# A fused delta-rule attention and MLP kernel: another order at the beginning, weights fetched at once and split in another way, the first two units' layers run jointly by halves of the weights

## The chip, the cores and the metric

The kernel runs on one core of a Trainium2 chip. The metric is the device time of one execution in microseconds, median over runs. The engines of the core are named as in the profile: PE (TensorE matmuls; PEld its weight loads), DVE (VectorE), ACT (ScalarE), POOL (GpSimd) and SP (SyncE, which issues most DMAs).

## The reference

For each batch and head a state of 48 x 48 is updated token by token by the delta rule, and the outputs go through two dense layers with a squared ReLU between them:

```python
k_n = k / (np.linalg.norm(k, axis=-1, keepdims=True) + 1e-06)
for t in range(S):
    kt, vt, bt = (k_n[:, :, t], v[:, :, t], beta[:, :, t, None])
    y[:, :, t] = np.einsum('bhd,bhde->bhe', q[:, :, t], state)
    v_old = np.einsum('bhde,bhd->bhe', state, kt)
    state = state + bt[:, :, :, None] * np.einsum('bhd,bhe->bhde', kt, vt - v_old)
h = np.maximum(x @ w_in, 0.0)          # x: y with its heads joined, (3072, 384)
return (h * h @ w_out).astype(np.float32)
```

There are 4 batches, 8 heads, 768 tokens and a head width of 48. `w_in` is 384 x 2048 and `w_out` 2048 x 384, both of 64-bit floats; q, k, v and beta are 32-bit. 12.6 MB of weights have to be read and turned into 32-bit numbers.

## The kernel before

**Units.** The work is cut into 12 units: 128 tokens of two batches, unit u being the token block u // 2 of batch pair u % 2. Inside a unit the tokens come in chunks of 64, and the token recurrence of a chunk is replaced by the inverse of a triangular matrix. Units of the same pair follow each other through `state`; the first two units (0 and 1) begin with a state of zero.

**What a unit goes through.** `load`, `load_v`, `load_q`, `load_beta` fetch its tokens over SP. `normalize` scales k. `static` transposes k and q and forms the masked products `ap`, which go through DRAM (`blocks`) into the layout `lt`. `invert` solves 31 steps on DVE, one pair of operations each (L347, L350), and sends the result over DRAM (`inv`) into `tt` and `t1t`. `whole` joins the halves of the inverse, `applied` multiplies it with k and v, and `sequential` carries the state over the two chunks and writes y. `moe` feeds y transposed into `x_h`, `x_l` (the number as a rounded part and a remainder, since the matmuls take rounded fp32), runs the first layer in 8 double blocks of 256 columns (two pieces of 9 matmuls each, L665), takes relu, square and the two parts on ACT and DVE (L672 to L675, `h_l` L644), and the second layer two double blocks later (two pieces of 6 matmuls of 384 each, L652), accumulated in the two banks `o0` and `o1`.

**Weights.** There are 28 parts: for each quarter of the 2048 columns three of `w_in` (128 x 512) and four of `w_out` (128 x 384). `split_weights` turns the two 32-bit words of each 64-bit number into a rounded high part and a rest: ACT takes the absolute value of the upper word (L145), DVE runs five operations (L146 to L154), ACT rounds the high part (L160), PE forms number minus high part plus lower bits as a sum of three matmuls (L165 to L167), and ACT copies it back as the rest (L168). The low step of one weight is written behind the high step of the next.

**Order.** The order of PE, SP, DVE and ACT is written out by hand: each part of the work is a generator, `take` runs some steps of one, and `weave` mixes several by positions between 0 and 1, with the layers as filler between steps of attention. The program begins with `first_pair` (units 0 and 1 together, with halves of 16 steps in the solve and products written into unused weight tiles), splits placed between its steps by `take(splits, 1)`; then `applied` and `sequential` of both units; then one `weave` per unit u from 1 to 11. Weave u has `static` of u + 1 in its first fifth, the state part of u from 0.34 on, most of `invert` of u + 1 from 0.40 on, the layers of u - 1 throughout, and in u = 1 the rest of the splits up to 0.88. SP's queue is in the order written, too. Weights are fetched in pieces between q, v and k of the first units, the last 13 (L130 by `fetch(NW)`) once the tiles that `first_pair` borrowed are free.

Of the kernel before, what the change touches and what calls it, by code (L numbers as in the profile page):

```python
# [16 lines left out]
LEAST = 2.0 ** -15  # L17
# [3 lines left out]
def kernel(  # L21
# [74 lines left out]
    ttall = const.tile([P, NU, NC, H, C], F32, name="tt")  # L96
    ttile = [ttall[:, i] for i in range(NU)]
# [24 lines left out]
    AHEAD = 10  # L122
# [10 lines left out]
    def room(x, n):  # L133
        pool, first, second = rooms[x % 2 if x < AHEAD else 0]
        return pool.tile([P, PC], I32, name=first)[:, :n], pool.tile([P, PC], I32, name=second)[:, :n]

    def split_weights():


        def words(x):  # L140
            raw = raws[x]
            w1 = raw[:, :, 1]
            a, rest = room(x, w1.shape[1])

            nc.scalar.activation(out=a.bitcast(F32), in_=w1.bitcast(F32), func=AF.Abs)  # L145
            nc.vector.tensor_scalar(out=a.bitcast(F32), in0=a.bitcast(F32), scalar1=LEAST, scalar2=None, op0=ALU.max)  # L146
            nc.vector.tensor_scalar(out=a, in0=a, scalar1=3, scalar2=0x3FFFFFF8,
                                    op0=ALU.logical_shift_left, op1=ALU.bitwise_and)

            nc.vector.scalar_tensor_tensor(out=a, in0=w1, scalar=-0x40000000, in1=a,  # L150
                                           op0=ALU.bitwise_and, op1=ALU.bitwise_or)

            nc.vector.tensor_scalar(out=w1, in0=a, scalar1=-0x800000, scalar2=None, op0=ALU.bitwise_and)  # L153
            nc.vector.scalar_tensor_tensor(out=rest.bitcast(F32R), in0=raw[:, :, 0].bitcast(U32), scalar=2.0 ** -52,  # L154
                                           in1=w1.bitcast(F32), op0=ALU.mult, op1=ALU.mult)
            return x, a, rest

        def high(x, a, rest):
            hl = wpool.tile([P, 2, raws[x].shape[1]], F32R, name=place[x])
            nc.scalar.copy(out=hl[:, 0], in_=a.bitcast(F32))  # L160
            return x, a, rest, hl

        def low(x, a, rest, hl):
            ps = split_bank()[:, :hl.shape[2]]
            nc.tensor.matmul(ps, lhsT=ident, rhs=a.bitcast(F32), start=True, stop=False)  # L165
# [3 lines left out]
            halves[weight_parts[x][:2]] = hl[:, 0], hl[:, 1]  # L169
# [160 lines left out]
    def invert(d):  # L330
# [21 lines left out]
        nc.vector.tensor_tensor(out=z, in0=z, in1=bt.unsqueeze(1).broadcast_to([P, J, HB]), op=ALU.mult)  # L352
        inv = dram.tile([4, H2, HB, HB], F32, name="inv")
# [12 lines left out]
    def first_pair(ds):  # L366
# [6 lines left out]
        chs = [(i, c, 2 * p + j, j, i * NX + c * NP + p) for i in range(2) for c in range(NC) for p in range(NP) for j in range(2)]  # L373

        def wide(x, *shape):
            return wpool.tile([P, *shape], F32, name=place[x])

        def all_heads(t):
            return ttall[:, :, :, :, t].rearrange("p u c h t -> p (u c h) t")

        bt = apool.tile([P, 2, HS], F32, name="btp", bufs=1)
        for r in range(2):
            for j in range(2):
                for half in range(2):
# [13 lines left out]
        yield

        def transposed(d, c, which):  # L400
            tp = x_tile(0).rearrange("p (n t) -> p n t", n=NP)
            for p in range(NP):
                nc.tensor.transpose(tp[:, p], d["qp" if which else "kp"][:, c, 2 * p:2 * p + 2].rearrange("p a b -> p (a b)"),
                                    ident)
            nc.scalar.copy(out=d["kq"][:, c, :, :, which], in_=tp.rearrange("p n (b t) -> p n b t", b=2))

        def blocks(across):

            ps = [x_tile(0).rearrange("p (i t) -> p i t", t=HB) for _ in range(2)]
            for i, d in enumerate(ds):  # L410
                for x in range(NX):
                    for half in range(2):
                        for r in range(2):
                            for j in range(2):
                                block = d["kq"][j * C:j * C + D, x // NP, x % NP, r, 0].rearrange("d (f t) -> d f t", f=2)
                                nc.tensor.matmul(ps[j][quarter[2 * r + half], i * NX + x], lhsT=block[:, half],
                                                 rhs=block[:, half ^ across], start=True, stop=True)
            return ps

        for d in ds:  # L420
            for c in range(NC):
                transposed(d, c, 0)
        yield
        near = blocks(0)
        yield
        f = apool.tile([P, 2, HS, 2, HS], F32, name="lt", bufs=1)
        gs = wide(NW - 7, 2, 2 * NX, HB)
        for j in range(2):
# [5 lines left out]
        for j, ps in enumerate(blocks(1)):  # L434
            nc.scalar.copy(out=os[:, j], in_=ps)
        yield
        for d in ds:
            for c in range(NC):
                transposed(d, c, 1)
# [419 lines left out]
```

## Time and profile before

| what | value |
|---|---|
| time, median of 3 runs | 744.1 us (741.33 to 745.07) |
| profiled execution, its own time | 744.84 us |
| its span, first to last instruction | 743.1 us |
| mean granted TensorE clock | 0.931 |
| PE busy | 660.0 us (89%) |
| DVE busy | 429.0 us (58%) |
| ACT busy | 335.2 us (45%) |
| POOL busy | 48.1 us (6%) |

Busy time is the union of an engine's instructions. Matmuls are pipelined and their ends are modelled, so a busy PE is not always a PE at its peak, and shares over the whole span mix stages with different limits; the granted clock of a slice tells of PE's pace there. In a group of instructions the fields are line, engine, operation, out<-in by tile names, shape, count, busy us and mean ns of one, and the idle time just before them with what ended it.

### The profile page before, as it was taken

How to read it: one execution, taken by the hardware profiler on the slowest of the kernel's cores; microseconds unless marked ns; L12 is line 12 of the kernel's file. 1: busy time of each engine (PE TensorE's matmuls, PEld its weight loads, DVE VectorE, ACT ScalarE, POOL GpSimd, SP SyncE). 2: the span in 40 equal slices, each digit the busy share in tenths (PEclk: the TensorE clock that was granted, in tenths of full speed). 3: DMA queues.
4: the chain of work that ended last, by engine and by line, in shares of the span. 5: the costliest groups of instructions: out<-in, count | busy, mean ns of one | idle time of the engine just before them, and what ended most of it. 6: DMA issues, size and time to landing. Idle time of an engine off the chain costs nothing.

```text
span 743.1 us, 25321 instructions
## 1 busy us (share of the span) xinstructions
PE 660.0 (89%) x11000; PEld 610.3 (82%) x11000; DVE 429.0 (58%) x1168; ACT 335.2 (45%) x623; POOL 48.1 (6%) x85
## 2 busy tenths in 40 slices
PE   2626876787689999999999999999999999999997
PEld 2415755566579999999999999999999999999997
DVE  3585146447774675764937748558476494661211
ACT  3321443544445535455444454553545534545352
POOL 8321100000001001010010100100101001000000
PEclk9775578788699999999999999999999999999999
DMA  8672700050003415324153142341532414111000
GB/s 176 168 182 53 279 6 2 4 93 12 1 1 65 94 26 100 54 46 98 28 100 67 26 98 49 52 100 25 105 57 36 99 35 93 33 29 32 3 21 21
DMA packets 164462, 47.71 MB, mean 64 GB/s; under 512 B 156416, under 2 KB 159488, under 8 KB 164352
## 3 DMA queue, kind: packets, MB, share of 16 engines
q1 hardware_dynamic: 160992, 45.48, 29.5%
q8 instruction: 86, 1.41, 0.8%
q10 hardware_dynamic: 2336, 0.59, 0.4%
q0 software_dynamic: 1024, 0.03, 0.1%
q14 instruction: 24, 0.20, 0.1%
HBM read 36.01 MB, written 9.96 MB: 62 GB/s over the span
## 4 chain that ended last, share of the span: by engine, by line
PE 80%; DVE 11%; ACT 4%; issue 3%; DMA 1%; SPq 0%; DVEq 0%; ACTq 0%
PE h L665 28%; PE o L652 27%; PE g L572 3%; PE g L596 3%; PE x L565 2%; PE x L609 2%; PE g L617 2%; PE o L165 1%; DVE a L150 1%; PE x L295 1%; DVE rest L154 1%; PE g L295 1%; DVE w L153 1%; PE g L285 1%; PE x L285 1%
## 5 line engine op out<-in xcount | busy, mean ns | idle before, releaser
L652 PE MATMUL o<-w,h_h 128*128 128x384 f32 x768 | 202.6, 345 | 0.0
L665 PE MATMUL h<-x_h,w 128*128 128x256 f32 x1152 | 177.5, 291 | 4.0 <-ACT w L168 3.1
L665 PEld LDWEIGHTS h<-x_h,w 128*128 128x128 f32 x1152 | 158.2, 194 | 10.0 <-ACT w L168 3.4
L644 DVE TENSOR_TENSOR h_l<-r,h_h 128x512 fp32r<-128x512 f32 x96 | 66.3, 691 | 149.4 <-PE o L652 68.6
L652 PEld LDWEIGHTS o<-w,h_h 128*128 128x128 f32 x768 | 133.2, 189 | 2.3
L672 ACT ACTIVATE r<-h 128x512 f32<-128x512 f32 x96 | 57.4, 598 | 171.3 <-PE h L665 171.0
L652 PE MATMUL o<-w,h_l 128*128 128x384 f32 x384 | 129.6, 337 | 0.0
L347 DVE SCALAR_TENSOR_TENSOR tmp<-lt,bt,z 128x126 f32<-128x126 f32 (+22 forms) x310 | 95.5, 308 | 23.6 <-DMA out_dram<-a 11.9
L665 PE MATMUL h<-x_l,w 128*128 128x256 f32 x576 | 101.1, 285 | 0.0
L350 DVE TENSOR_TENSOR z<-z,tmp 128x126 f32<-128x126 f32 (+22 forms) x310 | 79.2, 255 | 10.6
L665 PEld LDWEIGHTS h<-x_l,w 128*128 128x128 f32 x576 | 83.9, 194 | 0.0
L652 PEld LDWEIGHTS o<-w,h_l 128*128 128x128 f32 x384 | 72.2, 188 | 0.0
L673 ACT ACTIVATE r<-r 128x512 f32<-128x512 f32 x96 | 60.6, 632 | 3.1
L675 ACT CAST h_h<-r 128x512 fp32r<-128x512 f32 x96 | 59.5, 620 | 3.0
L160 ACT CAST w<-a 128x384 fp32r<-128x384 f32 (+1 forms) x23 | 12.7, 553 | 80.7 <-DVE rest L154 80.7
L338 POOL MEMSET z<- 128x512 f32 x10 | 5.3, 526 | 534.5 <-DMA inv<-z 478.0
L596 PEld LDWEIGHTS g<-state,kq 48*64 48x64 f32 x1408 | 24.3, 142 | 9.1 <-ACT a L145 4.5
L596 PE MATMUL g<-state,kq 48*64 48x48 f32 x1408 | 27.0, 228 | 5.1 <-ACT a L145 4.4
L146 DVE TENSOR_SCALAR a<-a 128x384 f32<-128x384 f32 (+1 forms) x23 | 8.8, 385 | 39.2 <-ACT a L145 39.2
L165 PE MATMUL x<-a,plus 128*128 128x384 f32 (+1 forms) x36 | 18.4, 597 | 13.3 <-DVE a L150 9.7
L240 DVE TENSOR_REDUCE n<-rest 128x8 f32<-128x384 f32 x20 | 10.9, 550 | 28.9 <-ACT rest L239 28.9
L551 ACT ACTIVATE tt<-x 32x256 f32<-32x256 f32 x40 | 15.0, 374 | 25.7 <-PE x L547 25.3
(171 smaller groups left out, 816.3 us busy)
## 6 DMA issues: line engine op xcount, KB each, us to landing
w<-in_moe_w_in_dram SPq DMA_DIRECT2D x12, 512.0 KB
w<-in_moe_w_out_dram SPq DMA_DIRECT2D x16, 384.0 KB
lt<-blocks SPq DMA_DIRECT2D x20, 256.0 KB
vt<-in_v_dram SPq DMA_DIRECT2D x96, 48.0 KB
out_dram<-a SPq DMA_DIRECT2D x46, 96.0 KB
kpad<-in_k_dram SPq DMA_DIRECT2D x88, 48.0 KB
qpad<-in_q_dram SPq DMA_DIRECT2D x88, 48.0 KB
blocks<-ap SPq DMA_DIRECT2D x40, 64.0 KB
```

The costliest lines, as they stand in the source:

```text
L165: nc.tensor.matmul(ps, lhsT=ident, rhs=a.bitcast(F32), start=True, stop=False)
L347: nc.vector.scalar_tensor_tensor(out=tmp, in0=lt[:, s:s + 1, s + 1:].broadcast_to([P, nj, nt]), scalar=bt[:, s:s + 1], op0=ALU.mult, op1=A ...
L350: nc.vector.tensor_tensor(out=z[:, :nj, s + 1:], in0=z[:, :nj, s + 1:], in1=tmp, op=ALU.subtract)
L551: nc.scalar.mul(out=right[upper[b], j, :, HB:], in_=ps[j][upper[b]], mul=-1.0)
L572: nc.tensor.matmul(g[rows, c, h], lhsT=tt[rows, c, h], rhs=vt[rows, c, h], start=True, stop=True)
L596: nc.tensor.matmul(dst[to * C:(to + 1) * C, j, p], lhsT=kq[rows, c, p, b, x], rhs=s[rows, b, p], start=(x == 0 and p == 0), stop=False, sk ...
L644: nc.vector.tensor_tensor(out=h_l, in0=r, in1=h_h.bitcast(F32), op=ALU.subtract)
L652: nc.tensor.matmul(o[i], lhsT=a[:, e, i * P:(i + 1) * P], rhs=halves["wo", ft][w], start=(ft == 0 and n == 0), stop=(ft == FT - 1 and n == 2))
L665: nc.tensor.matmul(hp[:, e], lhsT=halves["wi", (kt, ft // EACH)][w][:, f], rhs=x[:, kt], start=(n == 0), stop=(n == 3 * KT - 1))
L672: nc.scalar.activation(out=r, in_=hp, func=AF.Relu)
L673: nc.scalar.activation(out=r, in_=r, func=AF.Square)
L675: nc.scalar.copy(out=h_h, in_=r)
```

## The change

**Tiles.** `tt` is no longer a constant but a tile of the attention pool, made anew by `new_tt`: once for units 0 and 1, then its place holds `x1` (the layers' input of unit 1), then it is made again in the last step of `invert` of unit 2. The places of `first_pair` move out of the weights' tiles into others (`vt`, `h_h`, `x_h`, `x_l`), so no weight's fetch waits for them.

**Fetch.** All weights are issued on SP before v of units 0 and 1: 4 after k, 3 after q of unit 0, the rest after q of unit 1. v follows once `inner` has read the places it shares.

**Split.** ACT's step (`begin`) is issued two weights ahead and scales down, which replaces the `max` on DVE and lets one sign bit be merged instead of two. The first 6 weights still take PE's sum, with 4 operations on DVE. For the other 22, six operations on DVE form the rest directly, and PE and the second copy on ACT go.

```diff
-    ttall = const.tile([P, NU, NC, H, C], F32, name="tt")
-    ttile = [ttall[:, i] for i in range(NU)]
+    ttile = []
+
+    def new_tt():
+        tt = apool.tile([P, NU, NC, H, C], F32, name="tt", bufs=1)
+        ttile[:] = [tt[:, i] for i in range(NU)]
+        return tt
...
     def split_weights():
...
+        def words(x, sums):
+            a, rest = started[x]
+            n = a.shape[1]
+            w0, w1 = [raws[x][:, :, i] for i in range(2)]
+            nc.vector.tensor_scalar(out=a, in0=a, scalar1=3, scalar2=0 if sums else 1,
+                                    op0=ALU.logical_shift_left, op1=ALU.bitwise_or)
+            nc.vector.scalar_tensor_tensor(out=a, in0=w1, scalar=-0x80000000, in1=a,
                                            op0=ALU.bitwise_and, op1=ALU.bitwise_or)
...
+            else:
+
+                nc.vector.tensor_scalar(out=rest, in0=w0, scalar1=9, scalar2=None, op0=ALU.logical_shift_right)
+                nc.vector.scalar_tensor_tensor(out=rest, in0=w1, scalar=23, in1=rest,
+                                               op0=ALU.logical_shift_left, op1=ALU.bitwise_or)
+                hl = wpool.tile([P, 2, n], F32R, name=place[x])
+                power = apool.tile([P, PC], I32, name="t1", bufs=1)[:, :n]
+                nc.vector.tensor_scalar(out=power, in0=a, scalar1=-0x800000, scalar2=None, op0=ALU.bitwise_and)
+                nc.vector.scalar_tensor_tensor(out=hl[:, 1], in0=rest, scalar=2.0 ** -43, in1=power.bitcast(F32),
+                                               op0=ALU.mult, op1=ALU.mult)
             nc.scalar.copy(out=hl[:, 0], in_=a.bitcast(F32))
...
         before = None
+        begin()
+        begin()
+        yield
         for x in range(NW):
-            now = high(*words(x))
-            yield
+            sums = x < SUMS
+            now = words(x, sums)
             if before:
                 low(*before)
+            before = now if sums else None
+            if x + 2 < AHEAD:
+                begin()
+            if x >= AHEAD - 3:
                 yield
-            before = now
-        low(*before)
-        yield
...
+            if x + 2 >= AHEAD:
+                begin()
+            yield
```

**First pair.** It is cut into functions that are called one by one with `piece` (a split) between them. `blocks(1)`, the second pass of 256 small products, goes: `products` now multiplies k with k and q at once, and `outer` takes the block from `ap`. Beta comes by 8 DMAs and a transpose instead of 32. The masks of `ap` on POOL come after `outer`, and POOL's order is written by hand too.

**Joint layers.** The layers of units 0 and 1 run in four runs over halves of the weights: unit 0 with the first half (its sums are copied to `kept`, a tile in one of the two places of `vt`), unit 1 with the first and then the second half, and unit 0 with the second half, where `kept` is added. Of its 68 steps 50 stand in weave 1 and the rest in weave 2; weave 3 goes on with unit 2 alone as before. `invert` of unit 2 stands wholly in weave 1, from 0.5 to 0.9, and the rest of the splits up to 0.66.

```diff
+    def joint(d0, d1, x0, x1, kept):
+
+        def keep(o):
+            nc.scalar.copy(out=kept[:, 0], in_=o[0])
+            nc.vector.tensor_copy(out=kept[:, 1], in_=o[1])
+            yield
+
+        first, second = list(range(FT // 4)), list(range(FT // 4, FT // 2))
+        return layers([(d0, x0, first, keep), (d1, x1, first, None), (d1, x1, second, lambda o: results(d1, o)),
+                       (d0, x0, second, lambda o: results(d0, o, kept))])
...
+        x1 = apool.tile([P, 2, KT, 2 * P], F32R, name="tt", bufs=1)
+        x1 = [x1[:, 0], x1[:, 1]]
+        take(feed(ds_[1], x1))
         take(third)
-        split_early = False
+        kept = apool.tile([P, 2, DM], F32, name="vt", bufs=2)
         before = inverse = None
+        both = joint(*ds_[:2], x0, x1, kept)
         n_i = round((1 - I0) / (I1 - I0) * NI)
+        NJ, NF, NS = 68, 50, 2 * (NW - AHEAD + 3) - 16
         for u in range(1, units):
-            parts = [(splits, NS, 0, 0.88, "quiet")] if u == 1 else []
+            parts = [(splits, NS, 0, 0.66, "quiet")] if u == 1 else []
...
+            if u == 1:
+                parts.append((both, NF, M0, M1, ""))
+            elif u == 2:
+                parts.append((both, NJ - NF, 0, M1, ""))
```

**How the order moves.** On PE, where the first layer begins, before: `gy` of unit 1's state (L617), the sums of one weight (L165 to L167: number, high part, lower bits), then the 9 matmuls of a piece.

```order
L617 MATMUL g<-r,ap 64x48 x16
L165 MATMUL x<-a,plus 128x384
L166 MATMUL x<-w_1636,minus 128x384
L167 MATMUL x<-rest,plus 128x384
L665 MATMUL h<-x_h,w_296 128x256
L665 MATMUL h<-x_h,w_436 128x256
L665 MATMUL h<-x_h,w_451 128x256
```

And now, with the transposes of y of unit 1 (L668) in place of the sums:

```order
L654 MATMUL g<-r,ap 64x48 x16
L668 MATMUL h<-plus,y 128x128 x6
L735 MATMUL h<-x_h,w_282 128x256
L735 MATMUL h<-x_h,w_364 128x256
L735 MATMUL h<-x_h,w_447 128x256
```

The three matmuls of the sum are gone from here on, and the feed of unit 1, which stood in weave 2, has moved ahead of all layers.

On DVE, one weight of 384 columns in weave 1 and what stands next to it; before (`a` the words, `rest` the lower bits, `h_l` the remainder of the layers' middle values):

```order
L146 TENSOR_SCALAR a<-a 128x384
L147 TENSOR_SCALAR a<-a 128x384
L150 SCALAR_TENSOR_TENSOR a<-w_236,a 128x384
L153 TENSOR_SCALAR w_236<-a 128x384
L154 SCALAR_TENSOR_TENSOR rest<-w_236 128x384
L644 TENSOR_TENSOR h_l<-r,h_h 128x512
```

And now:

```order
L154 TENSOR_SCALAR a<-a 128x384
L156 SCALAR_TENSOR_TENSOR a<-w_202,a 128x384
L165 TENSOR_SCALAR rest<-w_202 128x384
L166 SCALAR_TENSOR_TENSOR rest<-w_202,rest 128x384
L170 TENSOR_SCALAR t_1722<-a 128x384
L171 SCALAR_TENSOR_TENSOR w_1721<-rest,t_1722 128x384
L704 TENSOR_TENSOR h_l<-r,h_h 128x512
```

One operation more stands ahead of the same `h_l`, and the last one writes the weight's rest itself.

On SP, v and q in weave 2 (units 3 and 4), with the semaphores each DMA waits for; before:

```order
L199 DMA kpad_102<-in_k_dram 64x4x48 [waits DMAHW6_49]
L199 DMA kpad_102<-in_k_dram 64x4x48 [waits DMAHW7_49]
L199 DMA vt<-in_v_dram 64x4x48 [waits DMAHW0_49]
L199 DMA vt<-in_v_dram 64x4x48 [waits DMAHW1_49]
L199 DMA vt<-in_v_dram 64x4x48 [waits DMAHW2_49]
```

And now:

```order
L215 DMA kpad_102<-in_k_dram 64x4x48 [waits DMAHW6_49]
L215 DMA kpad_102<-in_k_dram 64x4x48 [waits DMAHW7_49]
L215 DMA vt<-in_v_dram 64x4x48 [waits DMAHW0_49,DVE_49,Activation_49]
L215 DMA vt<-in_v_dram 64x4x48 [waits DMAHW1_49]
L215 DMA vt<-in_v_dram 64x4x48 [waits DMAHW2_49]
```

The order is the same, but the first DMA of v has a wait for DVE and ACT that it had not: of the two places of `vt` one is held by `kept`, and unit 2 uses the other.

More of the change, by code (lines that the diff above doesn't have):

```diff
@@ L513, in first_pair @@
[L513 to L522 removed]
+        return dict(betas=betas, sides=sides(), transposed=transposed, near=near, blocks=blocks, products=products,
+                    solve=solve(), inner=inner, joined=joined, halves_done=halves_done, outer=outer, last=last, masks=masks)
@@ L636, in moe, with xs_tiles, results, layers @@
             yield
-        o = [ps_o.tile([P, PC], F32, name=f"o{i}")[:, :DM] for i in range(2)]
-        hs, later = [], []
+    def xs_tiles():
+        return [mpool.tile([P, KT, 2 * P], F32R, name=n, bufs=1) for n in ("x_h", "x_l")]
+    def results(d, o, kept=None):
+        if kept is not None:
+            for c in range(2):
+                nc.vector.tensor_tensor(out=kept[:, c], in0=kept[:, c], in1=o[c], op=ALU.add)
+            done = [kept[:, c] for c in range(2)]
+        else:
+            done = []
+            for c in range(2):
+                done.append(spool.tile([P, PC], F32, name="a")[:, :DM])
+                (nc.vector.tensor_copy if c else nc.scalar.copy)(out=done[c], in_=o[c])
+        yield
+        for c in range(2):
+            for b in range(2):
+                row = (d["b0"] + b) * S + d["t0"] + c * C
+                queue = nc.scalar if d["u"] == units - 1 and c == 0 else nc.sync
+                queue.dma_start(out=out[row:row + C], in_=done[c][b * C:(b + 1) * C])
+    def layers(runs):
+        work = [(run, fp) for run in range(len(runs)) for fp in runs[run][2]]
+        later, o = [], []
         def rest():
@@ L644, in rest, with second @@
                 nc.vector.tensor_tensor(out=h_l, in0=r, in1=h_h.bitcast(F32), op=ALU.subtract)
-        def second(fp):
-            h_h, h_l = hs[fp]
+        def second(run, fp, h_h, h_l):
+            _, _, fps, end = runs[run]
+            if fp == fps[0] and (run == 0 or runs[run - 1][3]):
+                o[:] = [ps_o.tile([P, PC], F32, name=f"o{i}")[:, :DM] for i in range(2)]
+                begins = True
+            else:
+                begins = False
             for e in range(2):
@@ L652, in second @@
                         nc.tensor.matmul(o[i], lhsT=a[:, e, i * P:(i + 1) * P], rhs=halves["wo", ft][w],
-                                         start=(ft == 0 and n == 0), stop=(ft == FT - 1 and n == 2))
+                                         start=(begins and e == 0 and n == 0),
+                                         stop=(bool(end) and fp == fps[-1] and e == 1 and n == 2))
                 rest()
                 yield
-        for fp in range(FT // 2):
+            if end and fp == fps[-1]:
+                yield from end(list(o))
+        waiting = []
+        for run, fp in work:
+            x_h, x_l = runs[run][1]
             hp = ps_h.tile([P, PC], F32, name="h").rearrange("p (e t) -> p e t", e=2)
```

478 lines of the change are left out of this document (253 added, 225 removed).

## The prediction

> **What bounds the kernel now.** I read the page first, then the busy time by stretches. In the page's slices the granted TensorE clock is low and uneven over about the first twelve, and full after them:
>
> ```profile
> PEclk9775578788699999999999999999999999999999
> ```
>
> I cut the span at three places of the program: the first matmul of `applied` for unit 0, the first matmul of the first layer, and the end of the first weave (u = 1). The first two stand in the timeline of PE (start, length, line):
>
> ```profile
> 84.44 0.36 PE L565 MATMUL h<-tt,kpad 64*64 64x64 f32 x1
> ...
> 124.62 0.87 PE L665 MATMUL h<-x_h,w 128*128 128x256 f32 x6
> ```
>
> Busy time in these stretches (length, then each engine's busy us and count, the clock, DMA share and GB/s):
>
> ```profile
> 0.00:84.40 84.40, 40.64 (x1460) 33.03 (x1460) 43.51 (x90) 26.54 (x50) 30.56 (x58) 0.72 0.63 164
> 84.40:124.60 40.20, 31.04 (x675) 24.02 (x671) 19.59 (x46) 16.94 (x33) 0.00 (x0) 0.70 0.16 55
> 124.60:226.60 102.00, 76.32 (x420) 63.20 (x419) 68.04 (x171) 45.00 (x89) 0.00 (x0) 0.85 0.11 20
> 226.60:743.10 516.50, 511.98 (x8454) 490.02 (x8452) 297.85 (x861) 246.68 (x452) 17.59 (x27) 1.00 0.31 57
> ```
>
> Call them A, B, C and D. D is TensorE's alone: 512.0 of 516.5 us at clock 1.00. A, B and C last 226.6 us, with PE busy for 148.0 and below full clock; no engine is full there, chains through PE, ACT and DVE set the pace. So the change can gain in two ways: less work in D, or shorter chains in A to C.
>
> **Prices.** Warm matmuls and the period of the steady stage, from the chain of waits (start, us, what):
>
> ```profile
> 247.82 1.85 PE g L572 x64
> ...
> 264.25 2.11 PE o L652 x12
> ...
> 275.54 2.12 PE h L665 x18
> ...
> 296.33 1.85 PE g L572 x64
> ```
>
> A unit has 144 first-layer and 96 second-layer matmuls: 144/18 x 2.12 + 96/12 x 2.11 = 33.9 us, or 1.06 us for each of its 32 pieces. The period is 296.33 - 247.82 = 48.5 us, so attention takes 14.6.
>
> **D, work taken out.** What stood before the cut at 226.6 is seen in C's groups of matmuls, and in PE's timeline just before it:
>
> ```profile
> L665 PE MATMUL h<-x_l,w 128*128 128x256 f32 x51 | 10.9, 333 | 0.0
> ...
> L652 PE MATMUL o<-w,h_l 128*128 128x384 f32 x31 | 10.6, 343 | 0.0
> ```
>
> ```profile
> 223.10 0.60 PE L285 MATMUL g<-plus,qpad 128*128 128x128 f32 x4
> ```
>
> At 3 and 2 to a piece these are 17 first-layer and 16 second-layer pieces (one record is missing): 33 of 384 are done, 351 left, 372 us. The change's first weave runs 50 of the 68 steps of the joint layers, one of them the copy to `kept`, so 49 pieces; 335 are left, 355 us. That is 17 less in D, paid for in C; but unit 3's transposes, four groups like the row above, some 2 us, fall into D now. So -15.
>
> **C, the first weave.** PE's own work there is now 49 x 1.06 = 52 plus about 6 for `static` of unit 2 (part of the 14.6): 58. A weight's split cost it this (a cold one, then a warm one, each with the matmul that follows):
>
> ```profile
> 105.70 2.07 PE L165 MATMUL o<-r,plus 128*128 128x512 f32 x2
> ...
> 108.65 0.25 PE L609 MATMUL x<-r,kpad 64*64 64x48 f32 x1
> ...
> 163.86 0.81 PE L165 MATMUL x<-a,plus 128*128 128x384 f32 x2
> ...
> 164.86 0.34 PE L652 MATMUL o<-w,h_h 128*128 128x384 f32 x1
> ```
>
> So 1.00 to 2.95 us, for all 28 weights; now 6 have it. In C the splits leave PE altogether, and with them PE's waits for ACT's and DVE's half of each. The price goes to DVE, whose groups in C, shapes apart, read (count | busy, mean ns):
>
> ```profile
> L150 DVE SCALAR_TENSOR_TENSOR a<-w,a 128x384 int32<-128x384 int32 x11 | 6.1, 558 | 0.4
> ...
> L150 DVE SCALAR_TENSOR_TENSOR a<-w,a 128x512 int32<-128x512 int32 x6 | 4.2, 693 | 0.2
> ...
> L153 DVE TENSOR_SCALAR w<-a 128x384 int32<-128x384 int32 x11 | 4.0, 361 | 0.4
> ...
> L153 DVE TENSOR_SCALAR w<-a 128x512 int32<-128x512 int32 x6 | 2.6, 428 | 0.2
> ...
> L304 DVE TENSOR_TENSOR ap<-x,mask 128x512 f32<-128x512 f32 x2 | 1.3, 682 | 0.0
> ```
>
> ```profile
> L347 DVE SCALAR_TENSOR_TENSOR tmp<-lt,bt,z 128x126 f32<-128x126 f32 (+22 forms) x31 | 9.5, 306 | 0.5
> L350 DVE TENSOR_TENSOR z<-z,tmp 128x126 f32<-128x126 f32 (+22 forms) x31 | 7.9, 255 | 1.1
> ...
> L644 DVE TENSOR_TENSOR h_l<-r,h_h 128x512 fp32r<-128x512 f32 x8 | 5.5, 690 | 8.3 <-PE o L652 7.4 <-ACT h_h L675 0.8
> ```
>
> An old split is 2 such STTs and 3 TENSOR_SCALARs: 2.20 us (384) or 2.67 (512). A new one without sums is 3 and 3: 2.76 or 3.36. The shifts have no row; as TENSOR_SCALARs of the same shape I give them L153's. So the "fewer operations" hold for PE and ACT, not for DVE. Twelve weights (four of 512, eight of 384) remain for C: 13.4 + 22.1 = 35.5. To it come 13 `h_l` x 0.69 = 9.0, four masks of 0.68 = 2.7, the inversion of unit 2, now whole in C (17.4), and some 4 for norms and copies: about 69 against PE's 58. The weave puts the splits into its first 0.66 and the inversion into 0.5 to 0.9, so up to 0.66 DVE has 35.5 + 6 + 2.7 + 7 = 51 against PE's 38, then PE's 20 bounds: 71. I take 78, a tenth more for hand-overs. Bounds: 62 if DVE runs ahead, 97 if PE keeps its old ratio of 61 us of such work (35 layers, 20 splits, 6 static) in 102.
>
> **A, the beginning.** Rows of DVE and POOL around the solve:
>
> ```profile
> 39.32 0.36 DVE L146 TENSOR_SCALAR r<-r 128x384 f32<-128x384 f32 x1 [5.71 <-ACT r L145]
> ...
> 44.87 1.01 DVE L471 TENSOR_TENSOR z<-z,tmp 128x30 f32<-128x30 f32 x1
> ...
> 51.53 0.29 DVE L471 TENSOR_TENSOR z<-z,tmp 128x128 f32<-128x128 f32 x1
> ```
>
> ```profile
> 43.24 5.08 POOL L454 TENSOR_SCALAR_AFFINE_SELECT ap<-ap 64x1024 f32<-64x1024 f32 x4 [17.82 <-ACT ap L451]
> ```
>
> The 5.71 us before the fourth weight goes, since `begin` now starts its ACT step two weights ahead and before the q copies. While POOL masks `ap`, DVE steps of the solve take about 1 us that take 0.2 to 0.3 later; four of them, 3.4 us. The masks now come after `outer`, so that goes too. Four weights before the solve lose one TENSOR_SCALAR each: 1.6. After the solve one six-operation split more stands ahead of `halves_done`: +2. A = 84.4 - 5.7 - 3.4 - 1.6 + 2 = 76. Bounds: 86 if none of the three is gained, 70 if the pass of `blocks(1)`, which goes too, held the chain up (an estimate of 6, from A's 40.6 us of PE work).
>
> The Trainium skill (SBUF — State Buffer, "Who interferes with whom") says that a DVE instruction with two SBUF inputs contends with a GpSimd one that reads SBUF. The rows above agree. By it the masks hit the splits beside `last` instead, and the 3.4 us would come back there: A 79.
>
> **B, the states.** Six splits leave PE, half-way between cold and warm 2.0 us each: -11.9. `feed` of unit 1 comes in: +2. But PE waits there behind weights already:
>
> ```profile
> PE g L596 <- ACT a L145: 4.4, 1, 4.4
> ...
> PE h L609 <- DVE x_l L635: 3.2, 1, 3.2
> ```
>
> Now longer splits stand ahead of the state additions on DVE, and their ACT casts ahead of the copies of y; two more waits of a split and its cast, 4 each: +8. B = 38; bounds 30 with no such wait, 46 with four.
>
> The Trainium skill (TensorE: Matmul & The Clock Gate, "What's actually happening") has the clock fall to half after an idle window of about 3.4 us. The row of B, 0.70, fits a mixture. With the splits gone PE idles more; at half clock B's other 19 us of PE work at 0.70 become 27 and B 46.
>
> **Back in D.** Unit 2 has 15.9 + 14.6 = 30.5 us of PE work, with most of the next inversion (15), state steps, norms and results on DVE, some 24 in its last 60% (18 us): +4 in all, as some of it slips into unit 3. `kept` holds one of the two `vt` buffers until unit 0's results are out, so the v of unit 3 waits for unit 2's last use of v, at 0.84 of its weave, where it went out at about a third. Queued behind it on SP are q and beta of unit 4 and the inverse of unit 3:
>
> ```profile
> 157.71 5.21 SPq L199 DMA_DIRECT2D vt<-in_v_dram  x8
> 163.01 5.24 SPq L199 DMA_DIRECT2D qpad<-in_q_dram  x8
> 168.30 5.33 SPq L221 DMA_DIRECT2D bt<-in_beta_dram  x8
> ...
> 226.62 1.30 SPq L355 DMA_DIRECT2D inv<-z  x2
> ...
> 233.40 1.97 SPq L363 DMA_DIRECT2D t1t<-inv  x4
> ```
>
> About 16 us of issue from some 6 before unit 2's end; `static` wants q 2.5 us into unit 3, `whole` wants t1t at about 17, and 11 pass from inv to t1t's landing. I charge +5 (0 to 12). D = 516.5 - 15 + 9 = 510.5, bounds 501 and 522.
>
> **Sum.** 76 + 38 + 78 + 510.5 = 702.5 us of span, against 743.1. The profiled execution took 744.84, 1.7 more than its span and 0.7 above the median of the runs: 704.
>
> **Rivals.**
> 1. PE paces the first weave. For it: six-operation splits wait for nothing on PE any more, and a first run and a second need only weights that are split already. Against: the 69 us above. C 62, D without the 9, 501.5; A 74 and B 36: 673.5, with 1.7 for what lies around it 675.
> 2. The chains keep C at its old pace, 97, since ACT and DVE still work in order with PE. For it: in C no engine was over 75% busy. C 97 for 78: 704 + 19 = 723.
> 3. Slower: v behind the weights. All 28 weights now go out on SP ahead of v of units 0 and 1.
>
> ```profile
> w<-in_moe_w_in_dram SPq DMA_DIRECT2D x12, 512.0 KB
> w<-in_moe_w_out_dram SPq DMA_DIRECT2D x16, 384.0 KB
> ...
> ```
>
> ```profile
> 60.00:80.00 20.00, 15.99 (x671) 13.48 (x664) 7.72 (x14) 6.22 (x11) 1.89 (x2) 0.50 0.38 120
> ```
>
> That is 12.6 MB, with k, q and v about 15. At 120 GB/s v would land at 125, `applied` start 49 later than I say, and the time be 753. Down to 200 GB/s it is hidden (15 MB in 75 us); it makes the whole slower below about 130. For it: the rate of 60 to 80. Against: that stretch holds waits of SP, not a full queue.
>
> **How the numbers follow.** Forecast 0.50, rival 1 0.22, rival 2 0.20, rival 3 0.05, and 0.03 for a null. The likeliest one's own range is 690 to 718; the range of 675 to 732 takes in most of rivals 1 and 2. A change of 0.5% is about what can be told here: faster 0.92, within it 0.03, slower 0.05.
>
> **What would show it.** First-layer matmuls from about 114 us; DVE 85% busy or more from there to about 192, with PE waiting for `h_l` and for little else; 10 periods of nearly 48.5 after that, the third unit's with PE idle for some 10 us behind DMA of q or t1t. A first weave under 65 us speaks for rival 1, over 90 for rival 2, a DMA wait before `applied` for rival 3. The forecast is wrong if C is not shorter than 90 or A and B together not shorter than 120.

## The result, and the profile after

| | before | after |
|---|---|---|
| time, median of the runs beside each other | 744.6 us (741.3 to 746.0) | 703.0 us (701.9 to 704.6) |
| ratio | | 0.945, 95% interval 0.941 to 0.949 |
| profiled execution, and its span | 744.84 and 743.1 us | 701.87 and 700.1 us |
| mean granted TensorE clock | 0.931 | 0.930 |

The forecast was 704. The time came out, but the parts did not: the stages in front are shorter than forecast and the rest is longer. Busy time of the changed kernel by stretches: A, B and C as in the prediction, then weave 2, weave 3 and the rest (length, then busy us and count of PE, weight loads, DVE, ACT and POOL, the clock, DMA share, GB/s):

```profile
0.00:70.30 70.30, 39.12 (x1209) 31.57 (x1209) 50.09 (x114) 31.89 (x64) 12.88 (x31) 0.76 0.72 218
70.30:106.00 35.70, 23.67 (x655) 21.07 (x653) 28.32 (x60) 16.89 (x34) 6.05 (x6) 0.64 0.12 20
106.00:179.50 73.50, 61.82 (x465) 60.03 (x465) 63.50 (x163) 40.41 (x73) 1.89 (x2) 0.92 0.15 28
179.50:218.60 39.10, 32.15 (x691) 29.52 (x691) 24.62 (x75) 12.73 (x25) 1.96 (x3) 0.89 0.35 67
218.60:277.00 58.40, 52.09 (x836) 49.22 (x837) 32.61 (x100) 23.41 (x43) 2.39 (x3) 0.87 0.36 63
277.00:700.10 423.10, 418.40 (x6808) 400.52 (x6805) 238.17 (x685) 202.30 (x369) 13.70 (x21) 1.00 0.29 55
```

A 70.3 (forecast 76), B 35.7 (38), C 73.5 (78), D 39.1 + 58.4 + 423.1 = 520.6 (510.5). In C, DVE is busy for 86% and PE for 84%. The groups of DVE there, shapes apart, answer to those of the prediction (count | busy us, mean ns | idle us before them and what ended it):

```profile
L704 DVE TENSOR_TENSOR h_l<-r,h_h 128x512 fp32r<-128x512 f32 x13 | 8.9, 683 | 6.6 <-ACT h_h L745 3.9 <-PE o L717 2.7
L171 DVE SCALAR_TENSOR_TENSOR w<-rest,t 128x384 fp32r<-128x384 int32 x8 | 4.5, 558 | 0.3
...
L165 DVE TENSOR_SCALAR rest<-w 128x384 int32<-128x384 int32 x8 | 2.8, 354 | 0.0
...
L171 DVE SCALAR_TENSOR_TENSOR w<-rest,t 128x512 fp32r<-128x512 int32 x4 | 2.8, 692 | 0.1
...
L154 DVE TENSOR_SCALAR a<-a 128x512 int32<-128x512 int32 x4 | 1.7, 420 | 0.0
```

The shifts, which had no row before, cost what was assumed (354 ns for 384 columns). Three things in PE's timeline were to be explained (start, length, and in brackets the idle time before it and what ended it):

```profile
142.20 1.01 PE L717 MATMUL o<-w,h_h 128*128 128x384 f32 x2 [6.41 <-ACT vt L763]
...
218.64 1.12 PE L301 MATMUL x<-plus,kpad 128*128 128x128 f32 x4 [3.59 <-DVE state L649]
225.12 1.09 PE L301 MATMUL x<-plus,qpad 128*128 128x128 f32 x4 [5.36 <-DMA bt<-in_beta_dram]
```

The first is the copy into `kept` on ACT: `o` cannot be started anew before it, and it stands behind casts of weights that wait for DVE. The second is PE's wait for unit 2's state at the end of weave 2. The last is q of unit 4 (the profile names beta, which is issued right behind it; in run 2 it names q, 5.8 us). SP's queue in weave 2 shows why it is late:

```profile
196.32 6.63 SPq L215 DMA_DIRECT2D kpad<-in_k_dram  x8
213.44 5.21 SPq L215 DMA_DIRECT2D vt<-in_v_dram  x8
218.69 5.23 SPq L215 DMA_DIRECT2D qpad<-in_q_dram  x8
223.97 5.72 SPq L237 DMA_DIRECT2D bt<-in_beta_dram  x8
```

From 203.0 to 213.4 SP stands before v, which waits for the place in `vt` that `kept` does not hold; q and beta are issued after it.

### The profile page after: what moved, and what is told of

Same layout as the page of the kernel before. It is cut to its first block, busy times and chain, and to the rows that moved or that the text cites. A ratio compares the mean times of both kernels' runs of the same rounds, so it can differ in the third digit from the quotient of the medians.

```text
span 700.1 us, 24612 instructions
## 1 busy us (share of the span) xinstructions
PE 627.3 (90%) x10657; PEld 591.9 (85%) x10657; DVE 437.3 (62%) x1193; ACT 327.6 (47%) x606; POOL 38.9 (6%) x65
## 4 chain that ended last, share of the span: by engine, by line
PE 73%; DVE 14%; SPq 5%; issue 3%; DMA 2%; ACT 2%; DVEq 0%; ACTq 0%
PE h L735 27%; PE o L717 26%; SPq L215 4%; PE g L633 3%; PE g L609 2%; DVE tmp L363 2%; DVE z L366 2%; PE x L301 2%; PE x L646 2%; PE g L301 2%; PE x L311 1%; PE x L602 1%; PE g L311 1%; PE g L654 1%; DVE rest L166 1%
## 5 line engine op out<-in xcount | busy, mean ns | idle before, releaser
L735 PE MATMUL h<-x_h,w 128*128 128x256 f32 x1056 | 160.4, 288 | 1.5 <-ACT x_h L670 0.9
L735 PEld LDWEIGHTS h<-x_h,w 128*128 128x128 f32 x1056 | 141.6, 191 | 6.9 <-issue 1.8
L742 ACT ACTIVATE r<-h 128x512 f32<-128x512 f32 x96 | 57.4, 598 | 164.9 <-PE h L735 158.4
L735 PE MATMUL h<-x_l,w 128*128 128x256 f32 x528 | 91.6, 282 | 0.0
L735 PEld LDWEIGHTS h<-x_l,w 128*128 128x128 f32 x528 | 75.7, 191 | 0.0
L717 PEld LDWEIGHTS o<-w,h_l 128*128 128x128 f32 x384 | 72.8, 190 | 2.2 <-DVE h_l L704 2.2
L609 PE MATMUL g<-vt,tt 64*64 64x48 f32 x768 | 26.4, 225 | 0.3 <-ACT y L657 0.2
L609 PEld LDWEIGHTS g<-vt,tt 64*64 64x64 f32 x768 | 25.5, 142 | 0.5 <-ACT y L657 0.3
```

Of the source, the lines that this page charges most:

```text
L609: nc.tensor.matmul(g[rows, c, h], lhsT=tt[rows, c, h], rhs=vt[rows, c, h], start=True, stop=True)
L717: nc.tensor.matmul(o[i], lhsT=a[:, e, i * P:(i + 1) * P], rhs=halves["wo", ft][w], start=(begins and e == 0 and n == 0), stop=(bool(end) a ...
L735: nc.tensor.matmul(hp[:, e], lhsT=halves["wi", (kt, ft // EACH)][w][:, f], rhs=x[:, kt], start=(n == 0), stop=(n == 3 * KT - 1))
L742: nc.scalar.activation(out=r, in_=hp, func=AF.Relu)
```

## The experiments

Each is the changed kernel with one edit, unless it says otherwise. In the table, "weave 1 from" is the first transpose of unit 2's `static`, "to" that of unit 3's, and weaves 2 and 3 are counted likewise, all read from PE's timeline; B is "first layer" less `applied`, and C is "to" less "first layer". Later weaves take 48.5 to 49.0 in every run. The change and runs 1, 2, 4, 9 and 11 have the same instructions up to the first layer; among them `applied` lies between 69.2 and 71.3 and B between 35.7 and 36.6, so differences of that size in one profile show nothing.

| run | `applied` | first layer | weave 1 from | to | weave 2 | weave 3 | time, us |
|---|---|---|---|---|---|---|---|
| the kernel before | 84.4 | 124.6 | 125.7 | 221.8 | 49.5 | 48.5 | 744.6 |
| the change | 70.3 | 106.0 | 108.1 | 179.5 | 39.1 | 58.4 | 703.0 |
| 1 q ahead of v | 69.8 | 106.3 | 108.4 | 179.9 | 38.8 | 52.4 | 695.9 |
| 2 less inversion in weave 2 | 71.3 | 107.9 | 109.9 | 181.4 | 38.4 | 59.0 | 702.6 |
| 3 layers apart | 69.9 | 102.5 | 106.0 | 171.2 | 49.8 | 48.5 | 694.2 |
| 4 lighter splits | 69.2 | 105.7 | 107.8 | 171.0 | 38.9 | 57.3 | 694.0 |
| 5 ACT step not ahead | 75.9 | 113.5 | 115.6 | 187.2 | 39.6 | 58.8 | 710.6 |
| 6 the same, with the second pass | 82.6 | 120.9 | 123.0 | 193.4 | 40.1 | 56.9 | 716.2 |
| 7 masks early | 72.8 | 106.4 | 108.5 | 179.3 | 40.6 | 57.4 | 702.2 |
| 8 sums for 16 weights | 77.4 | 113.9 | 115.0 | 188.8 | 41.4 | 58.0 | 713.1 |
| 9 as 1, fewer pieces in weave 1 | 70.8 | 107.3 | 109.4 | 180.0 | 45.0 | 50.8 | 699.8 |
| 10 as 3, less inversion in weave 1 | 70.5 | 101.6 | 105.0 | 164.6 | 50.1 | 48.5 | 688.4 |
| 11 as 1, less inversion in weave 1 | 69.8 | 105.5 | 107.6 | 173.5 | 46.9 | 50.4 | 696.1 |
| 12 as 10, splits closer | 70.7 | 101.4 | 104.9 | 165.0 | 52.7 | 48.5 | 690.5 |

### What follows the first weave (1, 2)

```diff
-                load_v(ds_[u + 1])              # run 1, for u == 2
         load_q(ds_[u + 2]); load_beta(ds_[u + 2])
+                load_v(ds_[u + 1])
```

> In weave 2 alone, q and beta of unit 4 are issued ahead of v of unit 3 instead of behind it. In the changed kernel weave 2 runs from 179.5 to 218.6 (39.1 us), weave 3 from 218.6 to 277.1 (58.5, where the steady period is 48.5), and SP stands from 203.0 to 213.4 before the first DMA of v, with q behind it; PE then waits 5.4 us for q. Theory of the prediction (v is late because `kept` holds one of its two places, and what is queued behind it on SP comes late): weave 3 falls to 51 to 53.5, the whole to 696 to 698. Rival (DVE, with the inversion of unit 3 and the state steps, sets the pace there and the wait on SP is hidden): weave 3 stays within 1.5 of 58.5, the whole 701 to 704.

Weave 3 fell by 6.0, the whole to 0.934 of before (0.932 to 0.937). SP's queue of this run:

```profile
196.40 5.84 SPq L215 DMA_DIRECT2D kpad<-in_k_dram  x8
202.35 5.79 SPq L215 DMA_DIRECT2D qpad<-in_q_dram  x8
208.19 5.35 SPq L237 DMA_DIRECT2D bt<-in_beta_dram  x8
...
215.77 5.25 SPq L215 DMA_DIRECT2D vt<-in_v_dram  x8
```

v goes out at 215.8, 2.3 us later than in the changed kernel, and PE does not wait for it; it was what stood behind v that was late. That is the prediction's mechanism, priced at 5. Weave 3 of this run still lasts 3.9 longer than the later ones, and that is not waiting: PE is busy for nearly all of it, at a granted clock of 0.92.

```profile
218.70:271.10 52.40, 51.49 (x836) 49.06 (x837) 32.73 (x100) 23.36 (x43) 1.96 (x3) 0.92 0.36 65
```

```diff
-                parts.append((inverse, n_i, I0, 1, "quiet"))        # 27 steps, run 2 for u == 2
+                parts.append((inverse, 18, I0, 1, "quiet"))
```

> 18 of the 32 steps of unit 3's inversion stand in weave 2 instead of 27, the other 14 at the beginning of weave 3. Theory (weave 2 holds 18 steps of layers where other weaves hold 31, so DVE with 27 steps of inversion makes PE wait 2.3, 0.9 and 3.6 us for r and state): these waits fall to under 2 us together, weave 2 from 39.1 to 34 to 36, weave 3 stays or loses 1, the whole 698 to 700. Rival (the stall on SP before v decides, and the later end of the inversion makes t1t late in weave 3): weave 2 gains 3 to 5 and weave 3 loses as much, the whole 701 to 705.

Neither 34 to 36 nor a shift: weave 2 stayed at 38.4. Nine steps less on DVE gained nothing, so the sum of DVE's work doesn't set weave 2. DVE's timeline of this run shows what stands in the way:

```profile
206.83 0.55 DVE L256 TENSOR_REDUCE n<-rest 128x8 f32<-128x384 f32 x1 [2.18 <-ACT rest L255]
...
207.82 0.55 DVE L636 TENSOR_TENSOR r<-vt,g 128x384 f32<-128x384 f32 x1
```

`r` of unit 2's state, for which PE waits, stands on DVE behind the norm of unit 4's k, and DVE is idle there until the k that this needs is in. ACT's square of it:

```profile
206.28 0.94 ACT L255 ACTIVATE rest<-kpad 128x384 f32<-128x384 f32 x2 [3.98 <-DMA kpad<-in_k_dram]
```

Weave 2 is short, so what is fetched and used inside it arrives late. That reading was not tested, for instance by moving the norm.

### The first weave (3, 4)

```diff
-        take(feed(ds_[1], x1))
...
-                parts.append((both, NF, M0, M1, ""))
+                before = layers([(ds_[0], x0, list(range(FT // 2)), lambda o: results(ds_[0], o))])
+                parts.append((before, n_moe - OVER - 2, M0, M1, ""))
```

> The joint layers are undone and all the rest is kept: unit 0 alone in weave 1, its splits over 0.88 of the weave, unit 1 in weave 2 with its feed, no `kept`. Weave 1 then holds 27 pieces of layers instead of 49. Theory of the prediction (DVE paces the first weave; the joint order fills what PE has free there): weave 1 barely shorter than its 73.5 us, 66 to 74, 22 pieces x 1.06 = 23 us more come behind it, and some 12 are given back there, since v is not late and weave 2 has its full cover; the whole 706 to 716. Rival 1 (PE paces the first weave): weave 1 falls to 38 to 48, the whole stays within 3 of 703. Rival 2 (chains at the old pace): weave 1 at 85 or more, the whole above 720.

My theory was wrong in the result: apart, the kernel is 8.8 us faster (694.2 against 703.0). Most of that is the late q, which comes with `kept`: with run 1's order the joint layers take 695.9, so what they lose by themselves is 1.7, about the spread of the runs (694.8 to 696.6 joint, 693.4 to 695.5 apart). Busy time by the same stretches, first layer to the end of weave 1, then weaves 2 and 3:

```profile
102.50:171.20 68.70, 47.25 (x325) 43.71 (x321) 63.69 (x164) 31.06 (x57) 0.00 (x0) 0.82 0.16 30
171.20:221.00 49.80, 49.80 (x840) 47.78 (x839) 28.60 (x83) 23.82 (x44) 1.96 (x3) 0.97 0.34 63
221.00:269.50 48.50, 48.48 (x840) 46.26 (x839) 31.41 (x93) 23.68 (x44) 1.96 (x3) 1.00 0.35 65
```

C is 68.7 with 14.6 us less of PE's busy time and the same DVE work, 63.7: so far as forecast, DVE paces it. But weaves 2 and 3 together take 98.3, against 97.5 with 22 pieces fewer to do, or 91.2 in run 1: 7.1 less, for pieces that the prediction prices at 23. Apart they are full (PE 49.8 of 49.8); joint, PE is idle in them for 13.3 us, and busy only 14.0 us less, since its granted clock there is 0.89 and 0.87 instead of 0.97 and 1.00. And joint, C takes 4.8 more with DVE busy for as long. The row of `h_l` above has 6.6 us of waiting on DVE; here it reads:

```profile
L704 DVE TENSOR_TENSOR h_l<-r,h_h 128x512 fp32r<-128x512 f32 x8 | 5.5, 684 | 1.4 <-ACT h_h L745 1.4
```

With five more `h_l`, DVE, the full engine, waits 5.2 us more for ACT and PE; that this is what the 4.8 are is a reading, since the splits are spread in another way here, too. B is 3.1 shorter without the feed of unit 1.

```diff
+                if x < 16:      # else the words themselves stand for rest and power
                     nc.vector.tensor_scalar(out=rest, ...); nc.vector.scalar_tensor_tensor(out=rest, ...)
...
                     nc.vector.tensor_scalar(out=power, ...)
```

> The last 12 weights, those split in weave 1, leave out three of the six DVE operations (the two that form the lower word's bits and the one that masks the exponent), so the rest of these weights is another number. That takes about 4 x 1.6 + 8 x 1.4 = 17.6 us of work off DVE in weave 1 (64.0 us busy of 73.5) and nothing off PE (62.3 busy). Theory of the prediction (DVE paces weave 1): PE becomes its bound, 61 to 66 us, the whole 691 to 696. Rival 1 (PE paces it already): weave 1 73 to 74, the whole 702 to 704. Rival 2 (hand-overs between ACT, DVE and PE set the pace, not DVE's sum of work): weave 1 69 to 73, the whole 698 to 702.

DVE's busy time in C fell by 14.0, C to 65.3, and PE is busy for nearly all of it, at its bound:

```profile
105.70:171.00 65.30, 61.14 (x465) 60.32 (x465) 49.51 (x127) 40.73 (x73) 1.90 (x2) 0.94 0.18 31
```

So DVE paced weave 1; rivals 1 and 2 fall. That it is the sum of its work, and not the chain of each split, is told by run 10, where other work leaves DVE. Of PE's waits in C the one for `kept`, 6.41 us in the changed kernel, reads

```profile
PE o L721 <- ACT vt L767: 1.9, 1, 1.9
```

so most of it was DVE's lateness, seen through ACT.

### The beginning (5, 6, 7, 8)

```diff
-        begin()          # run 5: ACT's step of the first four where they are split
-        begin()
...
         p["blocks"]()
-        piece()
         for i in range(2):
             p["transposed"](i, 1)
+        piece()
```

> The first four weights take their ACT step when they are split and not two weights ahead, and the fourth is split behind the transposes of q, as in the kernel before; all the rest as in the changed kernel. There the solve's first step starts at 31.5 us (44.7 before) and `applied` of unit 0 at 70.3 (84.4 before). Theory of the prediction (the ACT step behind the copies of q held the solve up by 5.7 us): the solve starts at 36 to 39, `applied` at 75 to 78, the whole 707 to 711. Rival (the 13 us came from the second pass of small products that is gone, and the ACT step is hidden without it): the solve starts at 32 to 33.5, `applied` within 2 of 70.3, the whole 702 to 705.

> As the run before, and a second pass of 256 small products (32 x 32, high half against low half, two ACT copies that nothing reads) is put back on PE ahead of the transposes of q. Theory (both stood in one chain: pass, transposes of q, copies, ACT step, split, solve): the solve starts 6 to 7 us later than in the run before, at 42 to 45, `applied` at 80 to 84, the whole 712 to 718. Rival (the prediction's own account, where the pass has a cost of zero as the likeliest): the solve within 2 us of the run before.

Run 6 adds to run 5 the 256 small products and two copies on ACT that nothing reads, ahead of the transposes of q. Both theories hold for `applied` and for the whole; the solve begins somewhat later than either said (39.1 for 36 to 39, 46.3 for 42 to 45). The wait of DVE before the fourth weight, in run 5 and then in run 6, and the solve's first step in each:

```profile
33.06 0.36 DVE L154 TENSOR_SCALAR r<-r 128x384 int32<-128x384 int32 x1 [4.75 <-ACT r L147]
...
39.14 0.19 DVE L489 TENSOR_TENSOR tmp<-lt,z 128x30 f32<-128x30 f32 x1 [0.19 <-PE h L469]
```

```profile
40.25 0.36 DVE L154 TENSOR_SCALAR r<-r 128x384 int32<-128x384 int32 x1 [11.71 <-ACT r L147]
...
46.31 0.19 DVE L502 TENSOR_TENSOR tmp<-lt,z 128x30 f32<-128x30 f32 x1 [0.19 <-DVE lt L497]
```

The solve moved by 7.6 for the one and by 7.2 more for the other, `applied` by 5.6 and by 6.7 more: one chain from the pass to the solve, which the change cut at two places. With both back the solve begins 1.6 later than in the kernel before (44.7), so nothing else is needed for its earlier start.

```diff
                 p["products"](i, c)
                 take(p["solve"], 1 - c)
+            p["masks"](i)
...
-        for i in range(2):
-            p["masks"](i)
```

> POOL's masks of `ap` stand right behind the products again, under the solve, instead of behind `outer`. In the changed kernel the solve's 30 operations take 8.6 us (11.2 before), and the split operations from 68.0 to 77 take up to 1.50 us where others of the same shape take 0.35 to 0.69, some 4.7 us in sum, while POOL masks. Theory (the prediction's term: the masks slow the solve by 2.5 to 3.4, and the collision only moves): the solve's last step ends 2 to 3.5 later, `applied` at 72 to 74, the splits behind `applied` are back at their usual times and the stretch from `applied` to the first layer is 2 to 4 shorter; the whole 701 to 704. Rival (the collision behind `outer` is hidden under PE's own work, so the early one is a net loss): the second stretch stays at 35.7, the whole 705 to 708.

The collision moves and its price with it. In the changed kernel POOL's row and DVE's from 68.0 on:

```profile
68.46 5.58 POOL L555 TENSOR_SCALAR_AFFINE_SELECT ap<-ap 64x1024 f32<-64x1024 f32 x4
```

```profile
68.00 0.67 DVE L165 TENSOR_SCALAR h_l<-w 128x512 int32<-128x512 int32 x1
68.71 1.50 DVE L166 SCALAR_TENSOR_TENSOR h_l<-w,h_l 128x512 int32<-128x512 int32 x1
70.13 1.36 DVE L170 TENSOR_SCALAR t<-r 128x512 int32<-128x512 int32 x1
71.53 1.50 DVE L171 SCALAR_TENSOR_TENSOR w<-h_l,t 128x512 fp32r<-128x512 int32 x1
72.95 1.30 DVE L154 TENSOR_SCALAR a<-a 128x384 int32<-128x384 int32 x1
```

These five take 6.33 us; at the means of weave 1 (692, 420, 354 ns by shape and kind) they are 2.58. Early, the solve takes 12.3 us for 8.6 (8.6 in every other run of the changed kernel) and ends at 44.2 instead of 40.2; `applied` is 2.5 later and B 2.1 shorter: 702.2, no difference.

```diff
-    AHEAD, SUMS = 10, 6
+    AHEAD, SUMS = 10, 16
...
-            if x + 2 >= AHEAD:
-                begin()          # now one ahead, behind low of the weight before
```

> 16 weights instead of 6 take PE's sum of three matmuls with four DVE operations: all that are split ahead of weave 1. Each of the ten gives back 1.0 us of DVE and takes 1.0 to 2.9 of PE (warm to cold) and 0.5 to 0.6 of ACT; the ACT step of weights 10 to 15 is one weight ahead instead of two. Seven of the ten lie behind the start of `applied`, where in the changed kernel the stretch to the first layer is 35.7 us with PE busy for 23.7 and DVE for 28.3. Theory of the prediction (the sums were worth 11.9 us of that stretch): 43 to 47, `applied` at 71 to 74, the whole 710 to 717. Rival (DVE paces that stretch and PE has the room): 32 to 37, the whole 699 to 705.

The whole is in the theory's range, the places are not. B is 36.5, the rival's; the loss is in A, 7.1, between the solve's end and `applied` (36.8 us for 30.1). How much of it comes from the three sums there and how much from the ACT step that is now one weight ahead, this run doesn't tell. Of B and of the weave that follows:

```profile
77.40:113.90 36.50, 27.60 (x686) 21.17 (x681) 19.89 (x48) 17.73 (x37) 0.00 (x0) 0.86 0.02 5
113.90:188.80 74.90, 60.66 (x465) 58.28 (x463) 63.32 (x162) 40.56 (x74) 1.89 (x2) 0.95 0.15 27
```

In B seven sums cost 0.8 us, which is no more than B differs by without them, or 2.9 with the 2.1 of the masks, which lie ahead of `applied` here. With A's 7.1 it is 7.9 for ten sums. In B, DVE is busy for 8.4 less and PE's clock is 0.86 instead of 0.64.

### Toward a better order (9, 10, 11, 12)

```diff
-        NJ, NF, NS = 68, 50, 2 * (NW - AHEAD + 3) - 16
+        NJ, NF, NS = 68, 42, 2 * (NW - AHEAD + 3) - 16      # run 9, with the edit of run 1
```

> The first run of this study (q and beta of unit 4 ahead of v of unit 3), and 42 instead of 50 of the 68 joint steps in weave 1, so 26 instead of 18 in weave 2. That run had weave 1 at 71.5 us from transposes to transposes (DVE busy 63.5, PE 61.9), weave 2 at 38.8 (PE busy 32.2), weave 3 at 52.4, and 695.9 in all. Theory (weave 1 is paced by DVE, so taking 8.5 us of PE work out of it costs nothing there, and weave 2 has lost its filler, so PE waits for the state steps whatever DVE does): weave 1 66 to 70, weave 2 40 to 43, weave 3 49 to 52.5, the whole 690 to 694. Rival (weave 1 keeps its length, since its hand-overs and not DVE's sum set it, and weave 2 grows by the whole 8.5): the whole 699 to 704.

The rival's time: weave 1 gave back 0.9 (70.6 from 71.5), weave 2 grew by 6.2. Its reason, hand-overs, does not follow: DVE's busy time in C fell by 1.2 only (63.5 to 62.3), so a weave that DVE paces had as little to give. Pieces are not what weave 1 lasts for, and taking 7.5 us of PE's busy time out of it shortens next to nothing.

```diff
-                parts.append((inverse, NI if u == 1 else n_i, 0.5 if u == 1 else I0, 0.9 if u == 1 else 1, "quiet"))
+                parts.append((inverse, n_i, I0, 1, "quiet"))          # runs 10, 11 and 12
-        begin(); begin()
+        begin(); begin(); begin()                                     # runs 10 and 12
```

> The layers of the first two units apart (the third run of this study, 694.2: `applied` at 69.9, weave 1 65.2 from transposes to transposes with DVE busy 63.7 and PE 47.3, weave 2 49.8, weave 3 48.5), with 27 of the 32 steps of unit 2's inversion in weave 1 and 5 at the beginning of weave 2, as in the kernel before, and with the ACT step of the first ten weights three weights ahead instead of two (DVE waits 5.4 us for the seventh weight's at 49.8 to 55.3). Theory (DVE's sum of work paces weave 1, and weave 2 has room on DVE): weave 1 60 to 63.5, weave 2 49 to 51, `applied` at 67 to 69, the whole 686 to 691. Rival (weave 1 of this form is paced by the chain from split to layer and not by the sum): weave 1 64.5 to 66, the whole 691 to 695.

```profile
101.60:164.60 63.00, 47.40 (x324) 43.93 (x321) 58.75 (x149) 31.07 (x57) 0.00 (x0) 0.83 0.18 33
164.60:214.70 50.10, 49.74 (x840) 47.51 (x839) 33.15 (x100) 23.84 (x44) 1.96 (x3) 0.97 0.34 63
```

Five steps of inversion less on DVE, and weave 1 is 5.6 shorter; weave 2 takes them for 0.3. `applied` did not move: the ACT step a third weight ahead removes the wait of 5.4 us, but DVE then waits 3.7 for PE, and A gains nothing. At 688.4 this is the best of the kernels, 0.925 of before (0.923 to 0.928) and 14.6 us under the change.

> Joint layers as in the change, with q and beta of unit 4 ahead of v of unit 3, and 27 of the 32 steps of unit 2's inversion in weave 1 and 5 at the beginning of weave 2 instead of all 32 in weave 1. Compared with the first run of this study (695.9: weave 1 71.5 us with DVE busy 63.5, weave 2 38.8, weave 3 52.4), about 4 us of work leave DVE in weave 1. Theory (DVE's sum of work paces weave 1 whether the layers are joint or apart; apart the same move took it from 65.2 to 59.6): weave 1 66 to 69, weave 2 38 to 41, the whole 690 to 694, still above the 688.4 of the layers apart. Rival (weave 2, short of layers, gives the gain back, since the inverse of unit 2 now comes later there): weave 2 42 or more, the whole 695 to 698.

Weave 1 went to 65.9, as DVE's sum has it, and weave 2 to 46.9, as the rival has it: PE's waits there are

```profile
PE x L646 <- DVE r L636: 5.2, 2, 4.5
PE x L301 <- DVE state L649: 3.6, 1, 3.6
PE x L576 <- DMA tt<-inv: 3.5, 2, 2.6
```

The joint weave 2 has 18 steps of layers to put between these; I take that to be too few to cover them.

> The tenth run (688.4, layers apart, weave 1 59.6 us) with the splits of weave 1 over its first 0.76 instead of 0.88. The same operations in another order. Theory (DVE's sum of work, 58.7 us busy of 63.0, paces that weave): weave 1 within 1.5 of 59.6, the whole 687 to 690. Rival (the chain from a weight's split to the layer that needs it paces the end of the weave, where PE waits 3.1 us for a weight's cast): weave 1 55 to 58, the whole 683 to 687.

Weave 1 60.1 for 59.6: this change of the splits' order does not matter there. Weave 2 is 2.6 longer; PE waits 2.5 us in it for DVE's `x_l` (0.4 in run 10), and why that is late was not followed up.

## Why the prediction was right, and where it was not

- **A, 76 forecast, 70.3 measured.** The wait for the fourth weight's ACT step was 5.7 in the sum and 5.6 in run 5. The term that failed is the pass of `blocks(1)`: zero as the likeliest and 6 as the bound, it measured 6.7 (run 6). The +2 behind the solve is not shown: from its end to `applied` it is 28.6 before and 30.1 after, but 28.2 in runs 5 and 6 with the same splits there, and DVE waits 5.4 us in it for the ACT step of the seventh weight, which the prediction did not have. The masks' 3.4 are right as the price in the solve, 3.7 in run 7; 2.5 of it reached `applied`, and 2.1 came back in B. By the Trainium skill (SBUF — State Buffer, "Who interferes with whom") a DVE instruction with two SBUF inputs contends with a GpSimd one that reads SBUF. The rows above agree: 1.50 us for 0.69. From that rule the prediction worked out an A of 79; the collision did follow the masks to the splits, but most of it fell behind `applied`.
- **B, 38 forecast, 35.7 measured.** Near in sum, wrong in its terms, which is luck. -11.9 for six sums did not show: in the changed kernel seven put back cost 0.8 to 2.9 in B, and ten 7.9 in A and B together (run 8), 0.8 each where the prediction has 2.0. If so little came off, the +8 for longer splits is too high as well, as the sum came out. The feed was 3.1 (run 3), not 2. What did shorten B is not shown. In the kernel before, DVE waits 9.7 us up to 98.4, and 0.9 and 1.3 later in B, for ACT's step of a weight, and PE once 4.4; in the changed kernel DVE has no such wait in B. That the ACT step two weights ahead did it was not tested there, as run 5 undoes it for the first four weights only. By the Trainium skill (TensorE: Matmul & The Clock Gate, "What's actually happening") the clock falls to half after an idle window of about 3.4 us. With the half, the prediction worked out a B of 46. The clock did fall, 0.70 to 0.64, but B did not grow; it lasts 36.5 at 0.59 in run 9 and at 0.86 in run 8, so PE's clock does not set it.
- **C, 78 forecast, 73.5 measured.** The mechanism holds: DVE paces it (runs 4, 10, 11). Its operations add up to 69.4 us, against 69 in the sum (the splits 35.2 for 35.5, `h_l` 8.9 for 9.0); their records overlap, so that DVE is busy for 63.5 of the 73.5. The term that was off is the tenth for hand-overs, 7 on top of 71, where 2.5 came. C would have been 62 by rival 1 and 97 by rival 2. The first layer was to begin at 114 with DVE 85% busy to 192; it was 106, and 86% to 179.5. PE's longest wait in C, the 6.41 for `kept`, was not foreseen. What took C from 97.2 (by the marks of the table) to 73.5 is argued only: no run puts the sums back into weave 1.
- **D, 510.5 forecast, 520.6 measured.** The +5 for the late v, with q behind it on SP, measured 6.0 in weave 3 and 7.1 in all (run 1); PE was to be idle for some 10 us there and waited 5.4. The term that failed is the +4 for unit 2, laid to DVE: in weave 2 PE is idle for 39.1 - 32.2 = 6.9 us, 3.2 for `r` and 3.6 for `state`, and in run 1's weave 3, with 0.9 us of idle time left, PE is slower by 3.0 (51.5 us busy for 48.5, at a clock of 0.92 for 1.00). The sum of DVE's work is not the cause (run 2); where `r` stands in DVE's order may be. With that falls most of the use of the -15: against the layers apart, the 22 pieces that left D gained 0.8 there, or 7.1 with run 1's order, and cost 8.7 in front of D (179.9 for 171.2). By the marks of the table the kernel before has 521.3 in D: of the 43.0 us that the change gained in the profiles, A gave 14.1, B 4.5, C 23.7 and D 0.7.
- **Rival 3.** v went out at 52.0, PE waited for its DMA neither before `applied` nor in it, and the transfers ran at 296 GB/s from 20 to 40 us, with the weights among them, and at 393 from 30 to 50, not at 120:

```profile
20.00:40.00 20.00, 11.03 (x282) 8.15 (x280) 15.60 (x45) 11.05 (x22) 0.00 (x0) 0.90 0.87 296
```

A, B and C came out 5.7, 2.3 and 4.5 under, D 10.1 over. The time was met to 1 us because these nearly cancel, which is luck, and not because each was known.

## What to carry to other kernels

Work that is moved into a stage where its engine is idle gains only as much as the stage that it leaves gets shorter: what filled waits there leaves the waits behind. Here 23 us of layers left two weaves, which got 7.1 shorter at best, and what came before them got 8.7 longer. Price a stage by the engine that it lasts for, and take work from that engine (in the first weave five inversion steps on DVE were worth 5.6 us, eight pieces on PE 0.9). Where a tile is held longer, look in the in-order queue at what stands behind the transfer that waits for it.

## What was not expected of the hardware

A DVE operation with one tensor input was slowed by POOL's masks as much as those with two: 1.36 for 0.42 us, and 1.50 for 0.69. Each took about the length of one mask, 5.58 / 4 = 1.4 us. Undisturbed, the one-input operations are the faster kind: 128 columns more cost them 66 ns (420 less 354) and those with two inputs 134 (692 less 558). And adding PE work to a stretch can cost next to nothing there: with seven sums put into B, PE's busy time in it rose from 23.7 to 27.6 us, its granted clock from 0.64 to 0.86, and its length by 0.8.
